# Query and key rows by token tile, with the weights moving, and DMA transposes into head rows

## The chip, the cores and the metric

One NeuronCore of one Trainium2 chip. The metric is the device time of one execution in microseconds (us), from the launch of the kernel to its end; before the change it is 168.42 us, the median of 3 runs (167.94 to 169.54). The profile is of one execution of 168.68 us, in which the instructions span 166.7 us.

The engines are named as in the profile: PE multiplies matrices (PEld is its weight load), DVE and ACT work on vectors, POOL sets up constants, and SP issues most of the DMA transfers. Each runs its own list of instructions in order and waits on semaphores of the others.

## The reference

The input x has 2048 tokens of 448 values, in bfloat16. It is normalised (mean and variance of each token), and two branches read the normalised xn:

```python
# branch A: attention over a dilated window, 16 heads of 28
q, k, v = split(xn @ wqkv)                # [16, 2048, 28] each
idx = pos[:, None] - arange(8)[None] * 2  # 8 keys, every second token back
attn = softmax(where(idx >= 0, q . k[idx] / sqrt(28), -1e9))
s = merge_heads(attn . v[idx]) @ wo
# branch B: feed-forward, 448 -> 1792 -> 448
h = gelu(xn @ w1 + b1) @ w2 + b2
out = x + s * silu(h)
```

Only keys of the same parity are ever used, so the kernel holds the even tokens as positions 0 to 1023 and the odd ones as 1024 to 2047. In this order a query sees the 8 keys up to its own position.

## The kernel before, in words

**Tiling.** Tokens are in 16 tiles of 128 and 4 chunks of 512. The 448 values are contracted in three full tiles of 128 rows and a tail of 64. Two tails share the array at a time, one on its upper 64 rows and one on its lower, which `batch` (line 413) arranges: it closes up to two or more products with their tails and opens others with theirs, in one run of tail matmuls.

**Normalised tokens.** `norm` (390) makes xn for a tile; for the first 8 tiles PE transposes it, from tile 8 on a DMA transpose on the SP queue does it. The result is xnT, with the 448 values on partitions.

**Queries and keys.** `qk` (447) makes the rows for a group of four heads: the stationary operand is a piece of wqk, in which each head's 28 columns are padded to 32 (lines 348 to 357 copy the raw weights wraw into that layout), and the moving one is xnT, with up to 512 tokens. The bank then holds 4 heads x 32 rows by 512 tokens, and ACT or DVE copies it to qT or kT (462), of which there is one tile for each of four head groups. For chunk 0 the moving operand has 256 tokens, for the chunks 1 to 3 all 512.

**Values.** `vproj` (472) works the other way round: the stationary operand is a tile of xnT, the weights move, and tokens come out on partitions, in v_tok. `values` (489) makes the 128 keys of an attention block out of two such tiles by two DMA copies on SP.

**Attention.** `attn` (570) works in 17 blocks of up to 120 queries by 128 keys. The scores are 16 matmuls of 32 rows, which share the array four at a time (580); ACT takes the exponential (586), DVE multiplies with a mask (594), PE multiplies with the values (602), and DVE divides by the sum (609, 614) into os, a ring of three buffers. One or two DMA copies on SP put the block's rows into ot, a ring of four tiles of 128 tokens, and once a tile of tokens is complete a DMA transpose on SP turns it into oT (629).

**Feed-forward and end.** `ff1` (504) is 14 products a chunk with a gelu each, `ff2` (529) is 14 matmuls of 448 columns a tile, then a bias on DVE (552), a tanh on ACT (558) and a product on DVE (562). `final` (635) projects oT with wo, multiplies with the feed-forward branch, adds x and stores.

**What sets the order.** All work is entered as tasks with a cost, what they depend on, buffers they take and give back, and a priority. `_Plan.run` (79) goes through time with these costs and picks for the engine that is free earliest the task of highest priority within 0.12 us; this fixes each engine's list, which then runs in that order whatever the durations on the chip are. A DMA copy within the chip is entered with 0.55 us of SP (`dma_sb`, 309), a DMA transpose with 1.3 (`dma_T`, 315). The priorities are in the table PRIO (704). The chunks are entered in the order of line 739: the feed-forward and the attention of a chunk alternate, since the gelu and the exponential need different tables on ACT.

Of the kernel before, what the change touches and what calls it, by code (L numbers as in the profile page):

```python
# [11 lines left out]
ACT = mybir.ActivationFunctionType  # L12
# [141 lines left out]
def kernel(  # L154
# [46 lines left out]
    def sb(name, shape, dt=BF16):  # L201
        return const.tile(shape, dt, name=name)
# [13 lines left out]
    b1 = sb("b1", [P, NMT], F32)  # L216
    b2 = sb("b2", [P, D])
    xnT = sb("xnT", [P, KT, S])
    qT = [sb(f"qT{g}", [P, S]) for g in range(G)]
    v_tok = [sb(f"v_tok{t}", [P, H, 32]) for t in range(9)]  # L220
    v_tok = v_tok[8:] + v_tok[1:8] + v_tok[:8]
    kT = [sb(f"kT{g}", [P, S]) for g in range(G)]
    oT = sb("oT", [P, KT, S])
    ident = sb("ident", [P, P])
    eps_t = sb("eps_t", [P, 1], F32)
# [30 lines left out]
    def buf(pool, owner, i=0):  # L256
        return pool.bufs[owner.slots[pool][i]]
# [10 lines left out]
    def copy(e, o, i):  # L268
        if e == "ACT":
            nc.scalar.copy(o, i)  # L270
        else:
            nc.vector.tensor_copy(o, i)
# [174 lines left out]
    def qk(t0, t1, g, which, prio):  # L447
        cs = slice(t0 * P, t1 * P)
        n = (t1 - t0) * P
        hs = slice(H * which + 4 * g, H * which + 4 * g + 4)  # L450
        r = slice(64 * which, 64 * which + 64)
        dst, done = (kT, t_k) if which else (qT, t_q)

        def full(ps, kt, start, stop):
            nc.tensor.matmul(ps[:, :n], wqk[:, kt, hs, :], xnT[:, kt, cs], start=start, stop=stop)  # L455

        def tail(ps, start, stop):
            nc.tensor.matmul(ps[:, :n], wqk3[r, 4 * g:4 * g + 4, :], xnT[r, 3, cs], start=start, stop=stop)  # L458

        def evac(a, own, i):  # L460
            def fn(k):
                copy(k.on, dst[g][:, cs], buf(p_b, own, i)[:, :n])
            k = plan.add(("ACT", "DVE"), (act(n), dve(n)), fn, [a], prio + 2, give=((p_b, own, i),))
            for t in range(t0, t1):
                done[(g, t)] = k
        return _Job(n, full, tail, which, [t_xT[t] for t in range(t0, t1)] + t_wqk[:3], evac, (), t_wqk[3:])

    t_v, v_at, h_at = {}, {}, {}
    t_vt = {}
# [100 lines left out]
    def attn(b, prio, gate, early):  # L570
        q0, nq, k0 = BLK[b]
        m = m_b0 if b == 0 else m_sp if b == SPLIT else m_gen
        deps = [t_k[(g, c)] for g in range(G) for c in range(k0 // P, (k0 + P - 1) // P + 1)]
        deps += [t_q[(g, c)] for g in range(G) for c in range(q0 // P, (q0 + nq - 1) // P + 1)]

        def f1(k):
            for g in range(G):
                for hl in range(4):
                    r = slice(32 * hl, 32 * hl + 32)
                    nc.tensor.matmul(buf(p_b, k, hl)[:, g * nq:(g + 1) * nq], kT[g][r, k0:k0 + P],  # L580
                                     qT[g][r, q0:q0 + nq], start=True, stop=True)
        a = plan.add("PE", 0.15, f1, deps + early, prio, take=(p_b,) * 4, tail=0.15, mode=32)
        pv, exps = [], []
        for hl in range(4):
            def f2(k, hl=hl):
                nc.scalar.activation(buf(p_E, k)[:, :, :nq],  # L586
                                     buf(p_b, a, hl)[:, :4 * nq].rearrange("p (g q) -> p g q", g=4),
                                     ACT.Exp, scale=SCALE)
            e = plan.add("ACT", act(4 * nq), f2, [a] + gate + t_E, prio + 2, take=(p_E,), give=((p_b, a, hl),), table=("exp",))
            exps.append(e)  # L590

            def f3(_, e=e):
                E = buf(p_E, e)
                nc.vector.tensor_tensor(out=E[:, :, :nq], in0=E[:, :, :nq], in1=m[:, :, :nq], op=ALU.mult)  # L594
            w = plan.add("DVE", dve(4 * nq, 2), f3, [e] + t_mask, prio + 2)

            def f4(k, e=e, hl=hl):
                ps = buf(p_b, pv[0] if hl else k)[:].rearrange("p (h c) -> p h c", h=H)
                v = buf(*v_at[b]) if v_at[b] else v_tok[k0 // P]
                for g in range(G):  # L600
                    h = 4 * g + hl
                    nc.tensor.matmul(ps[:, h, :DH + 1], buf(p_E, e)[:, g, :], v[:, h, :DH + 1],  # L602
                                     start=True, stop=True)
            pv.append(plan.add("PE", 0.12, f4, [w] + t_v[b] + pv[-1:], prio + 3, take=() if hl else (p_b,),
                               give=((p_E, e, 0),) + ((v_at[b],) if hl == 3 and v_at[b] else ()), tail=0.15))
        po = pv[0]

        def f5(k):
            nc.vector.reciprocal(buf(p_rd, k)[:nq, :],
                                 buf(p_b, po)[:nq, :].rearrange("p (h c) -> p h c", h=H)[:, :, DH])  # L610
        r = plan.add("DVE", 0.25, f5, [pv[-1]], prio + 4, take=(p_rd,))

        def f6(k):
            nc.vector.tensor_tensor(  # L614
                out=buf(p_os, k)[:nq, :].rearrange("p (h c) -> p h c", h=H),
                in0=buf(p_b, po)[:nq, :].rearrange("p (h c) -> p h c", h=H)[:, :, :DH],
                in1=buf(p_rd, r)[:nq, :].unsqueeze(2).to_broadcast((nq, H, DH)), op=ALU.mult)
        o = plan.add("DVE", dve(D), f6, [r], prio + 4, take=(p_os,), give=((p_b, po, 0), (p_rd, r, 0)))
        q = q0
        while q < q0 + nq:  # L620
            t, row = divmod(q, P)
            n = min(P - row, q0 + nq - q)
            first, d = dma_sb(lambda k, t=t, row=row, n=n: buf(p_ot, ot_at.get(t, k))[row:row + n, :D],
                          lambda q=q, n=n: buf(p_os, o)[q - q0:q - q0 + n, :], [o] + t_os + [d for _, d in ot[t]],
                          () if ot[t] else (p_ot,), ((p_os, o, 0),) if q + n == q0 + nq else ())
            ot[t].append((first, d))
            ot_at[t] = ot[t][0][0]
            if row + n == P:
                t_oT[t] = dma_T(oT[:, :, t * P:(t + 1) * P], lambda t=t: buf(p_ot, ot_at[t])[:], [d for _, d in ot[t]],
                                (p_ot, ot_at[t], 0))  # L630
            q += n
        return exps
# [52 lines left out]
    for m, w, n, lo, hi in masks:  # L685
# [13 lines left out]
        def fn(_, m=m, w=w, n=n):  # L699
# [1 line left out]
        t_mask.append(plan.add("DVE", 0.3, fn, [t_m, t_st[3]], prio=60))  # L701


    PRIO = {"project": (77, 71, 71, 36.5),
            "attn": (922.5, 900, 875, 876),
            "ff1": (72.5, 91, 75, 75),
            "ff2": (63, 73, 3, 5),
            "final": (52.5, 36.5, 49.5, 49.5, 93.5, 82.5, 101.5, 48.5)}
    blocks_of = [[b for b, (q0, nq, _) in enumerate(BLK) if (q0 + nq - 1) // CH == c] for c in range(NCH)]
    gate = [early]  # L710

    def project(c):
        p = PRIO["project"][c]
        for t in range(c * TPC, (c + 1) * TPC):
            norm(t, 97 - 2 * t if t < TPC else p + 1)
        vs = [vproj(t, t % 2, p) for t in range(c * TPC, (c + 1) * TPC)]
        if c == 0:
            for i in range(0, len(vs), 2):
                batch(vs[i:i + 1], vs[i + 1:i + 2], 96 if i == 0 else p)
        for t0, t1 in ((0, 2), (2, 4)) if c == 0 else ((c * TPC, (c + 1) * TPC),):  # L720
            for g in (0, 2):
                batch(*[[qk(t0, t1, h, w, p) for w in range(2)] for h in (g, g + 1)], p)
        if c:
            batch(vs[:2], vs[2:], p - 0.1)
        for b in blocks_of[c]:
            values(b)

# [11 lines left out]
    for c, what in ((0, "F"), (0, "A"), (1, "A"), (1, "F"), (2, "A"), (2, "F"), (3, "A"), (3, "F")):  # L739
        if what == "A":  # L740
            exps = []
            for b in blocks_of[c]:
                exps += attn(b, PRIO["attn"][c], gate, gels)
            if c:
                gate = exps
        else:
            p = PRIO["ff1"][c]
            hs = [ff1(c, mt, mt % 2, p, gate) for mt in range(NMT)]
            batch(hs[0:2], hs[2:4], p)
            batch(hs[4:6], hs[6:8], p - 0.01)  # L750
            ff1_last[c] = batch(hs[8:10], hs[10:14], p - 0.02)
            gate = [t_h[(c, mt)] for mt in range(NMT)]
            gels = gate[:-1]
            if c == 0:
                gate = [rstds(8, 8, gate)]
                project(2)
                project(3)
            for t in range(c * TPC, (c + 1) * TPC):
                ff2(t, PRIO["ff2"][c])
    for t in range(NT):  # L760
        final(t, PRIO["final"][t // 2])

    plan.run()
    with tc.manual_schedule():
# [31 lines left out]
```

The softmax here doesn't subtract the row's maximum and nothing guards it: scores larger than these inputs give would overflow.

## Time and profile before

| what | value |
|---|---|
| time, median of 3 | 168.42 us (167.94 to 169.54) |
| span of the profiled execution | 166.7 us |
| DVE busy | 105.2 us (63%) |
| ACT busy | 110.3 us (66%) |
| matmuls for query and key rows, full, 512 columns | 68 x 379 ns = 17.2 us busy (line 455; the trace leaves out a few records) |
| their tails, 512 columns | 24 x 381 ns (line 458) |
| feed-forward 2 matmuls | 224 x 352 ns (line 536) |
| DMA engines, mean share busy by the main queue | 35.6% |

A row of the list of groups reads: line, engine, operation, what is written and read, shapes, count | busy time in us, mean ns of one | idle time of the engine ahead of them, and what ended it. A matmul's duration has its way through the array in it, and matmuls overlap, so the mean of one says less than the pitch at which they follow each other; the chain of work in order of time shows that. Its lines are: start, duration, what, and how many. SPq is SP's list of DMA issues; its durations are what an issue takes the queue, and not how long the data takes.

### The profile page before, as it was taken

To read this page: it belongs to the slowest core of one execution; us is meant where nothing else is said; L and a number is where in the kernel's file an instruction comes from. 1 tells how busy PE (TensorE), PEld (TensorE's weight loads), DVE (VectorE), ACT (ScalarE), POOL (GpSimd) and SP (SyncE) were. 2 spreads that over 40 slices of the span, in tenths; PEclk is the share of its full clock that TensorE was granted. 3 is DMA by queue.
4 is the path that set the end of the run, shared out by engine and by line. 5 is a ranking of instruction groups with operands and counts; after the bars stand their busy time and mean duration, and the time that the engine had idled before them with its cause. 6 is when DMAs were issued, how large, how long until landed. Compare 5 with 4: busy or idle time off the path is not lost.

```text
span 166.7 us, 3522 instructions
## 1 busy us (share of the span) xinstructions
PE 159.5 (96%) x1316; PEld 77.1 (46%) x1328; DVE 105.2 (63%) x278; ACT 110.3 (66%) x201; POOL 4.6 (3%) x29
## 2 busy tenths in 40 slices
PE   6999999999999999999999999999999999999980
PEld 2455534454454455433556533543466543345530
DVE  4789994087899968320196920694788987005762
ACT  3286469987888985698867798454895468851210
POOL 7300000000000000000000000000000000000000
PEclk9999999999999999999999999999999999999996
DMA  5999993024273233235313332022123244100101
GB/s 155 271 374 252 331 304 99 16 50 94 47 93 76 78 82 87 56 97 103 75 37 71 73 66 53 0 83 83 31 75 81 53 130 105 36 0 0 55 28 57
DMA packets 26520, 16.06 MB, mean 96 GB/s; under 512 B 14536, under 2 KB 25992, under 8 KB 26504
## 3 DMA queue, kind: packets, MB, share of 16 engines
q1 hardware_dynamic: 26072, 15.39, 35.6%
q10 hardware_dynamic: 432, 0.46, 0.9%
q8 instruction: 10, 0.16, 0.4%
q14 instruction: 6, 0.05, 0.1%
HBM read 7.06 MB, written 1.84 MB: 53 GB/s over the span
## 4 chain that ended last, share of the span: by engine, by line
PE 91%; DVE 3%; DMA 2%; issue 1%; SPq 1%; DVEq 0%
PE bank L536 25%; PE bank L510 20%; PE bank L455 13%; PE bank L639 7%; PE bank L477 6%; PE bank L602 4%; PE bank L513 4%; PE bank L285 4%; PE bank L580 3%; PE bank L458 3%; DMA ot<-os 2%; PE bank L405 1%; PE bank L480 1%; DVE sg L644 1%; DVE os L614 1%
## 5 line engine op out<-in xcount | busy, mean ns | idle before, releaser
L536 PE MATMUL bank<-w,h 128*128 128x448 bf16 x224 | 46.2, 352 | 0.0
L586 ACT ACTIVATE E<-bank 128x480 bf16<-128x480 f32 (+1 forms) x68 | 33.3, 577 | 10.7 <-PE bank L580 10.6
L510 PE MATMUL bank<-xnT,w 128*128 128x512 bf16 x160 | 38.4, 379 | 0.6 <-issue 0.3
L517 ACT ACTIVATE h<-bank,b 128x512 bf16<-128x512 f32 x56 | 34.3, 700 | 5.1 <-PE bank L513 5.1
L536 PEld LDWEIGHTS <-h 128*128 128x128 bf16 x224 | 20.6, 97 | 18.1
L510 PEld LDWEIGHTS <-w 128*128 128x128 bf16 x168 | 15.1, 97 | 21.6 <-issue 5.8
L455 PE MATMUL bank<-xnT,wqk 128*128 128x512 bf16 (+1 forms) x116 | 24.0, 336 | 0.3 <-issue 0.2
L594 DVE TENSOR_TENSOR E<-E,m_gen 128x480 bf16<-128x480 bf16 x60 | 22.3, 404 | 2.5 <-ACT E L586 1.6
L558 ACT ACTIVATE t<-y 128x448 f32<-128x448 f32 x16 | 9.3, 582 | 18.2 <-DVE y L552 18.1
L552 DVE TENSOR_TENSOR y<-bank,b 128x448 f32<-128x448 f32 x16 | 9.9, 621 | 13.5 <-PE bank L536 13.5
L644 DVE SCALAR_TENSOR_TENSOR sg<-bank,g 128x448 bf16<-128x448 f32 x16 | 9.9, 621 | 9.8 <-PE bank L639 9.2
L602 PEld LDWEIGHTS <-E 128*128 128x128 bf16 x272 | 11.4, 96 | 7.7 <-DVE E L594 0.8
L455 PEld LDWEIGHTS <-wqk 128*128 128x128 bf16 x120 | 10.4, 97 | 8.9 <-issue 2.1
L639 PE MATMUL bank<-wo,oT 128*128 128x448 bf16 x64 | 14.1, 352 | 0.1
L270 ACT CAST qT<-bank 128x512 bf16<-128x512 f32 (+1 forms) x17 | 8.5, 500 | 7.1 <-PE bank L458 5.6
L614 DVE TENSOR_TENSOR os<-bank,rd 120x448 bf16<-120x448 f32 (+1 forms) x17 | 10.6, 625 | 4.0 <-DMA ot<-os 3.4
L602 PE MATMUL bank<-v,E 128*128 128x29 bf16 x240 | 11.2, 176 | 0.0
L365 DVE BATCH_NORM_STATS2 st<-x_sb 128x6 f32<-128x448 bf16 x16 | 9.7, 603 | 1.9 <-DMA x_sb<-in_A_x_dram 1.8
L477 PE MATMUL bank<-wv,xnT 128*128 128x448 bf16 x48 | 10.8, 354 | 0.0
L562 DVE SCALAR_TENSOR_TENSOR g<-t,y 128x448 bf16<-128x448 f32 x16 | 9.9, 620 | 0.9 <-ACT t L558 0.7
L513 PE MATMUL bank<-xnT,w 64*128 64x512 bf16 x56 | 8.8, 380 | 0.1
L639 PEld LDWEIGHTS <-oT 128*128 128x128 bf16 x64 | 5.9, 97 | 5.2
(60 smaller groups left out, 116.0 us busy)
## 6 DMA issues: line engine op xcount, KB each, us to landing
out_dram<-o SPq DMA_DIRECT2D x16, 112.0 KB
w<-in_B_w_dram SPq DMA_DIRECT2D x1, 1568.0 KB
x_sb<-in_A_x_dram SPq DMA_DIRECT2D x3, 448.0 KB
w<-in_B_w_dram SPq DMA_DIRECT2D x1, 1344.0 KB
wraw<-in_A_wqkv_dram SPq DMA_DIRECT2D x1, 448.0 KB
w<-in_B_w_dram SPq DMA_DIRECT2D x2, 224.0 KB
x_sb<-in_A_x_dram SPq DMA_DIRECT2D x3, 112.0 KB
wo<-in_A_wo_dram SPq DMA_DIRECT2D x1, 336.0 KB
```

The source lines that it names most:

```text
L455: nc.tensor.matmul(ps[:, :n], wqk[:, kt, hs, :], xnT[:, kt, cs], start=start, stop=stop)
L477: nc.tensor.matmul(ps[:, :D], xnT[:, kt, k0:k0 + P], wv[:, kt, :], start=start, stop=stop)
L510: nc.tensor.matmul(ps[:], w1[:, kt, ms], xnT[:, kt, cs], start=start, stop=stop)
L513: nc.tensor.matmul(ps[:], w1[r, 3, ms], xnT[r, 3, cs], start=start, stop=stop)
L517: nc.scalar.activation(buf(p_h, own, i)[:], buf(p_b, own, i)[:], ACT.Gelu_apprx_tanh, bias=b1[:, mt:mt + 1])
L536: nc.tensor.matmul(ps[:, :D], buf(*h_at[(c, mt)])[:, j * P:(j + 1) * P], w2[:, mt, :], start=(mt == 0), stop=(mt == NMT - 1))
L586: nc.scalar.activation(buf(p_E, k)[:, :, :nq], buf(p_b, a, hl)[:, :4 * nq].rearrange("p (g q) -> p g q", g=4), ACT.Exp, scale=SCALE)
L594: nc.vector.tensor_tensor(out=E[:, :, :nq], in0=E[:, :, :nq], in1=m[:, :, :nq], op=ALU.mult)
L602: nc.tensor.matmul(ps[:, h, :DH + 1], buf(p_E, e)[:, g, :], v[:, h, :DH + 1], start=True, stop=True)
L614: nc.vector.tensor_tensor(out=buf(p_os, k)[:nq, :].rearrange("p (h c) -> p h c", h=H), in0=buf(p_b, po)[:nq, :].rearrange("p (h c) -> p h ...
L639: nc.tensor.matmul(ps[:, :D], oT[:, kt, t * P:(t + 1) * P], wo[:, kt, :], start=(kt == 0), stop=(kt == KT - 1))
L644: nc.vector.scalar_tensor_tensor(out=buf(p_sg, k)[:], in0=buf(p_b, a)[:, :D], scalar=0.5, in1=buf(p_g, t_g[t])[:], op0=ALU.mult, op1=ALU.mult)
```

## The change

From chunk 1 on, query and key rows are made in the way of the values. The stationary operand is a token tile of xnT, the raw weights wraw move with 448 columns, and a bank then holds 128 tokens by 16 heads x 28. ACT or DVE copies this into a staging buffer of 128 tokens by 16 heads x 32, whose last 4 columns of each head stay zero, and a DMA transpose on SP turns this into the four head groups' rows of 128 tokens. Staging buffers are the six halves of the wqk tile, which after chunk 0 nobody else needs. qT and kT become one tile each, since one transpose writes all four groups. It is to save columns: 448 in place of 512 for each of the matmuls, since the padding no longer passes through PE. Three chunks of 4 tiles with q and k give 24 more DMA transposes; the number of matmuls and of evictions is the same.

The priorities are new too, and finer: of their own for the values, for norm and for the second half of a projection, and by tile for ff2 and final.

```diff
-    qT = [sb(f"qT{g}", [P, S]) for g in range(G)]
+    qT = sb("qT", [P, G, S])
+    kT = sb("kT", [P, G, S])
...
-                copy(k.on, dst[g][:, cs], buf(p_b, own, i)[:, :n])
+                copy(k.on, dst[:, g, cs], buf(p_b, own, i)[:, :n])
...
+    p_qk = _Pool([wqk[:, kt, H * w:H * w + H, :] for kt in range(3) for w in range(2)])
+
+    def qk_rows(t, which, prio):
+        cs = slice(t * P, (t + 1) * P)
+        r = slice(64 * which, 64 * which + 64)
+        dst, done = (kT, t_k) if which else (qT, t_q)
+
+        def full(ps, kt, start, stop):
+            nc.tensor.matmul(ps[:, :D], xnT[:, kt, cs], wraw[:, kt, which * D:(which + 1) * D], start=start, stop=stop)
+
+        def tail(ps, start, stop):
+            nc.tensor.matmul(ps[:, :D], xnT[r, 3, cs], wraw3[r, :], start=start, stop=stop)
+
+        def evac(a, own, i):
+            def fn(k):
+                copy(k.on, buf(p_qk, k)[:, :, :DH], buf(p_b, own, i)[:, :D].rearrange("p (h c) -> p h c", h=H))
+            k = plan.add(("ACT", "DVE"), (act(D), dve(D)), fn,
+                         [a] + [d[g, 0] for d in (t_q, t_k) for g in range(G)] + [d[g, 2] for d in (t_q, t_k) for g in range(G)],
+                         prio + 2, take=(p_qk,), give=((p_b, own, i),))
+            m = dma_T(dst[:, :, cs], lambda: buf(p_qk, k).rearrange("p h c -> p (h c)"), [k], (p_qk, k, 0))
+            for g in range(G):
+                done[(g, t)] = m
+        return _Job(D, full, tail, which, [t_xT[t]], evac)
...
-    PRIO = {"project": (77, 71, 71, 36.5),
-            "attn": (922.5, 900, 875, 876),
-            "ff1": (72.5, 91, 75, 75),
-            "ff2": (63, 73, 3, 5),
-            "final": (52.5, 36.5, 49.5, 49.5, 93.5, 82.5, 101.5, 48.5)}
+    PRIO = {"project": (94.5, 86.5, 66, 41),
+            "attn": (98, 84.5, 65.5, 58.5),
+            "ff1": (94.5, 96.5, 104, 75.5),
+            "ff2": (64.5, 58, 68, 29.5, 80.5, 52, 44.5, 47, 8.5, 5.5, 2, 1.5, 77, 58, 110, 1),
+            "final": (57, 44.5, 9.5, 7.5, 94.5, 55, 84, 67.5, 77.5, 21.5, 75, 54, 16.5, 32.5, 130.5, 50),
+            "values": (15.5, 30.5, 23, 17),
+            "project2": (95.5, 76.5, 26.5, 26.5),
+            "norm": (79.5, 102.5, 10, 1)}
...
-        for t0, t1 in ((0, 2), (2, 4)) if c == 0 else ((c * TPC, (c + 1) * TPC),):
-            for g in (0, 2):
-                batch(*[[qk(t0, t1, h, w, p) for w in range(2)] for h in (g, g + 1)], p)
-        if c:
-            batch(vs[:2], vs[2:], p - 0.1)
+            for t0, t1 in ((0, 2), (2, 4)):
+                for g in (0, 2):
+                    batch(*[[qk(t0, t1, h, w, p) for w in range(2)] for h in (g, g + 1)], p)
+        else:
+            for t, q in ((c * TPC, p), (c * TPC + 2, PRIO["project2"][c])):
+                batch(*[[qk_rows(u, w, q) for w in range(2)] for u in (t, t + 1)], q)
+            batch(vs[:2], vs[2:], pv)
...
-                ff2(t, PRIO["ff2"][c])
+                ff2(t, PRIO["ff2"][t])
...
-        final(t, PRIO["final"][t // 2])
+        final(t, PRIO["final"][t])
```

More of the change, by code (lines that the diff above doesn't have):

```diff
@@ L218 @@
     xnT = sb("xnT", [P, KT, S])
-    qT = [sb(f"qT{g}", [P, S]) for g in range(G)]
+    qT = sb("qT", [P, G, S])
+    kT = sb("kT", [P, G, S])
     v_tok = [sb(f"v_tok{t}", [P, H, 32]) for t in range(9)]
     v_tok = v_tok[8:] + v_tok[1:8] + v_tok[:8]
-    kT = [sb(f"kT{g}", [P, S]) for g in range(G)]
     oT = sb("oT", [P, KT, S])
@@ L579, in f1 @@
                     r = slice(32 * hl, 32 * hl + 32)
-                    nc.tensor.matmul(buf(p_b, k, hl)[:, g * nq:(g + 1) * nq], kT[g][r, k0:k0 + P],
-                                     qT[g][r, q0:q0 + nq], start=True, stop=True)
+                    nc.tensor.matmul(buf(p_b, k, hl)[:, g * nq:(g + 1) * nq], kT[r, g, k0:k0 + P],
+                                     qT[r, g, q0:q0 + nq], start=True, stop=True)
         a = plan.add("PE", 0.15, f1, deps + early, prio, take=(p_b,) * 4, tail=0.15, mode=32)
@@ L712, in project @@
     def project(c):
-        p = PRIO["project"][c]
+        p, pv = PRIO["project"][c], PRIO["values"][c]
         for t in range(c * TPC, (c + 1) * TPC):
-            norm(t, 97 - 2 * t if t < TPC else p + 1)
-        vs = [vproj(t, t % 2, p) for t in range(c * TPC, (c + 1) * TPC)]
+            norm(t, 97 - 2 * t if t < TPC else PRIO["norm"][c])
+        vs = [vproj(t, t % 2, pv) for t in range(c * TPC, (c + 1) * TPC)]
         if c == 0:
             for i in range(0, len(vs), 2):
-                batch(vs[i:i + 1], vs[i + 1:i + 2], 96 if i == 0 else p)
-        for t0, t1 in ((0, 2), (2, 4)) if c == 0 else ((c * TPC, (c + 1) * TPC),):
-            for g in (0, 2):
-                batch(*[[qk(t0, t1, h, w, p) for w in range(2)] for h in (g, g + 1)], p)
-        if c:
-            batch(vs[:2], vs[2:], p - 0.1)
+                batch(vs[i:i + 1], vs[i + 1:i + 2], 96 if i == 0 else pv)
+            for t0, t1 in ((0, 2), (2, 4)):
[5 more added lines that the diff above has]
+            batch(vs[:2], vs[2:], pv)
         for b in blocks_of[c]:
```

## The prediction

> **What bounds the kernel now.** I read the page's busy times and the chain that ended last first, to see which engine sets the span.
>
> ```profile
> PE 159.5 (96%) x1316; PEld 77.1 (46%) x1328; DVE 105.2 (63%) x278; ACT 110.3 (66%) x201; POOL 4.6 (3%) x29
> ...
> PE 91%; DVE 3%; DMA 2%; issue 1%; SPq 1%; DVEq 0%
> ```
>
> PE is busy for all but 7 us, and 91% of the chain is PE. Of those 7 us, 1.2 lie ahead of the first matmul and about 5 behind the last one (from 161.7 to 166.7). What is left between is under 1 us. So a microsecond of matmul taken out is a microsecond of span, as long as nothing makes PE wait that doesn't now.
>
> Second, the chain in order of time, to price a matmul where it runs back to back.
>
> ```profile
> 20.20 0.54 PE bank L513 x4
> 20.74 2.69 PE bank L510 x12
> ...
> 147.51 3.97 PE bank L536 x21
> ```
>
> 21 matmuls of 448 columns take 3.97 us, 189 ns each. Twelve of 512 take 2.69 and the four half-height tails, which run in pairs, 0.54. With a 512 column matmul at 216 ns, twelve make 2.59 and two pairs 0.43, and about 0.1 us is left over in each piece: the price of going from one array tiling to another.
>
> Third, the groups with shapes kept apart, for the query and key rows that are replaced and for the evictions.
>
> ```profile
> L455 PE MATMUL bank<-xnT,wqk 128*128 128x512 bf16 x68 | 17.2, 379 | 0.3 <-issue 0.2
> L270 ACT CAST qT<-bank 128x512 bf16<-128x512 f32 x10 | 5.9, 590 | 5.7 <-PE bank L458 4.4 <-PE bank L455 1.0
> L270 ACT CAST v_tok<-bank 128x448 bf16<-128x448 f32 x9 | 4.8, 539 | 0.6 <-PE bank L480 0.5
> ```
>
> The v_tok row is the price of an eviction of the new kind: 448 columns out of a bank into 16 groups of 28.
>
> Fourth, the DMA queue of SP, since all that is added goes there: durations by tile, and its order of time.
>
> ```profile
> L317 SPq DMA_TRANSPOSE oT<-ot x16: 1190/1216/2109, 42.4 to 140.0; - x16
> ...
> L311 SPq DMA_DIRECT2D v<-v_tok x30: 510/716/1300, 22.5 to 123.0; - x30
> ```
> ```profile
> 34.64 5.23 SPq L317 DMA_TRANSPOSE xnT<-xn  x4
> ...
> 40.32 0.54 SPq L311 DMA_DIRECT2D ot<-os  x1
> 42.40 1.19 SPq L317 DMA_TRANSPOSE oT<-ot  x1
> ...
> 55.64 11.30 SPq L311 DMA_DIRECT2D v<-v_tok  x14
> ...
> 74.62 3.84 SPq L317 DMA_TRANSPOSE oT<-ot  x3
> ```
>
> A transpose holds the queue for 1.22 us and a copy for 0.72; with the gaps I use 1.25 and 0.74. From 34.6 to 80.4 us the queue's pieces add up to 40.4 of 45.8 us: PE is not the only thing that is nearly full. Its lateness already reaches an engine, in the list of waits:
>
> ```profile
> DVE os L614 <- DMA ot<-os: 3.4, 1, 3.4
> ```
>
> At 68.3 us DVE stood still for 3.4 us until a copy had freed an os buffer. PE was in a feed-forward stage then and did not need DVE, so it cost nothing.
>
> **What the Trainium skill says.** "TensorE: Matmul & The Clock Gate", section Back-to-back issue gap, gives N/2.4 + 2.5 ns for an isolated warm matmul and says that a real stream runs closer. Here the formula holds: it gives 189 ns for 448 columns (189 measured) and 216 for 512 (216 fits). "Perfetto Trace Analysis", section DMA Instruction — HWDGE (DVE, Sync), says that the profiler's window of such an instruction covers the sequencer and the descriptors, and not the movement of the data. The trace agrees: the first transpose is issued at 34.64, the DMA engines are empty until 35.85, and busy until 36.6, so it lands some 2.2 us after its issue began. "DMA: Bandwidth & Descriptors", section Issuing engines are not separate DMA queues, says that spreading DMAs over queues saves only issue time; no run here shows it, but issue time is what is scarce.
>
> **The change part by part.**
>
> *Matmuls.* A chunk has 24 full and 8 tail matmuls of 512 columns before, and as many of 448 after. A full one saves 64/2400 = 26.7 ns; the tails run in pairs, so count as 4. That is 28 x 26.7 = 0.747 us a chunk, 2.24 us for three. In the changed order PE goes from one tiling to another 88 times against 87, which gives 0.1 back. Gain: 2.14 us.
>
> *Evictions.* There are 24 either way. Before: 5.9 + 4.7 us on ACT (10 qT, 8 kT), 4.1 on DVE. After: 19 on ACT at 0.54 and 5 on DVE at 0.62, 13.4 against 14.7 us. Both engines have a third of the span free; I count nothing.
>
> *One tile for all head groups, the new weights.* The scores read the same 32 rows by 120 columns, and the raw weights have long landed, since the padded layout is copied out of them before its first use at 9.5 us: nothing.
>
> *Transposes on the DMA engines.* 24 of 0.13 MB. The four of 34.6 to 40.5 ran at about 220 GB/s, 0.6 us each, so 24 make 14 us over 90 us of span, beside engines that are a third busy: not a bound. Landing time: q and k of a tile come 2.2 us after the issue, before the evictions alone. The scores of block 4 stand in PE's order some 13 us behind the first of these evictions, so that is hidden.
>
> *Transposes on the SP queue.* This is the cost. Sixteen of them (chunks 1 and 2) fall into the stretch that was 40.4 of 45.8 us full, and 16 x 1.25 = 20 us don't fit. So what the queue did there slips. I walk the queue in the changed order, from the first xn transpose, which starts near 34.6 in both: the matmuls ahead of it are the same. Ahead of the transpose of the first attention output tile (oT 0) stand 24 transposes and 23 copies: 24 x 1.25 + 23 x 0.74 = 47.0, and 0.8 for the third xn, which DVE makes after a y and a mask product. So oT 0 is issued at 82.4 and lands at 84.6. Three more transposes, and at 86.2 to 86.9 the copy that lets go of os1; it lands some 1.4 us after its issue (40.86 to 42.40 is 1.5), at 88.3. The copy that lets go of os2 follows after a transpose and three copies, at 90.4, and lands at 91.8.
>
> PE, by the same prices and the changed order, counted from the start of feed-forward 0 at 18.91 + 0.93 (16 norm transposes of 58 ns now come ahead of it) and with what the same count falls short of the trace before (0.8 us at 60, 1.3 at 79): block 5's values are wanted at 59.8, output projection 0 at 84.0, the second head group's product of block 9 at 87.5. Against the queue:
>
> - Blocks 5 and 6 need value copies that stand 23rd and 24th in the queue, land at 60.4 and 61.2, and find PE at 59.8 and 60.5. PE waits about 1 us in all. Output projection 0 then comes at 85.0, just after oT 0.
> - DVE's order has block 7's normalisation into os1 ahead of a g and the mask product of block 9's second group. It waits to 88.3; os 0.65, g 0.6, product 0.4 end at 90.0. PE stands at 88.5: 1.5 us.
> - The same at os2: 91.8, then 0.6 and 0.4 give 92.8, PE at 92.0: 0.8. The products behind it cost 0.4 and 0.2.
>
> Then the queue has room: a block brings one transpose and two copies, 2.7 us, and PE takes over 4 for a block with its feed-forward work. In the last chunk I find no wait over 0.4, and leave it out. New waits: 1.0 + 1.5 + 0.8 + 0.6 = 3.9 us.
>
> *Priorities.* They only change the order, which the walk has in it. The end is the same in both orders (14 feed-forward matmuls, 8 of the projection, then DVE and the last store), so the 5 us tail stays.
>
> Sum: 168.42 - 2.14 + 3.9 = 170.2 us. The two bounds for the waits: nothing, if each copy finds 1 us of slack more at each place; and with a transpose at 1.6 us in a burst (two at 46.0 took 3.25) the queue is 24 x 0.35 = 8.4 us later at oT 0, of which PE, being later too, would feel 5 to 7 us in place of 3.9. I take the median prices, because most bursts show them.
>
> **The rivals.**
>
> *The queue keeps up.* PE gets its 2.14 us and waits for nothing: 166.3. For it: the new order puts the attention transposes and stores late and the q and k ones early, as if the queue had been reckoned with, and the 3.4 us wait of DVE before cost nothing. Against it: the 60 us of issue for 46 us.
>
> *The queue runs at burst prices.* 168.42 - 2.14 + 6.5 = 172.8. For it: transposes of 1.93 and 2.11 us in dense stretches. Buffers add to it: an eviction into one of the six staging buffers waits for a transpose six earlier, on ACT, with exponentials queued behind it, whose banks PE wants. Against it: of 24 transposes few are over 1.3.
>
> **How the numbers follow.** The late queue, 170.2, has 0.48; it spreads over 168.5 to 171.7. The queue that keeps up, 166.3, has 0.32, and burst prices, 172.8, 0.20. Faster by over 1% (below 166.7) is most of the second, 0.28; within 1% is the rest of it and the lower part of the first, 0.29; slower (above 170.1) 0.43. The range from 166.0 to 173.0 holds both rivals' middles.
>
> **What would show it.** Right: 48 transposes on SP at about 1.2 us, the queue without gaps from 35 to 85 us, PE busy near 157.3, DVE os waiting for ot copies between 80 and 95 us, with PE weight loads of E waiting for DVE there. Wrong: PE at its old 96% with 2 us less, so that the queue's lateness found slack; or PE waiting for kT or qT, which I hold to be in time; or ACT waiting at the staging buffers.

## The result and the profile after

The changed kernel takes 176.81 us (median of 4, 175.97 to 177.35) against 168.37 for the one before in the same comparison: a ratio of 1.0485, with an interval of 1.0418 to 1.0552. It is slower by 8.4 us, where 1.8 had been forecast, and outside the range. The profiled execution took 175.97 us, with a span of 174.2 us against 166.7. Here and below a time is the median of all executions, and a ratio leaves out the slow ones, which lie over 1.5% above the fastest of the same kernel.

The page of the kernel after: busy times, two rows of the 40 slices, the chain by engine, the two groups of matmuls that now stand still, and the new rows' full matmuls and evictions on ACT.

```profile
PE 159.8 (92%) x1320; PEld 77.1 (44%) x1328; DVE 103.3 (59%) x276; ACT 110.1 (63%) x203; POOL 4.5 (3%) x29
...
PE   7999999999999679999849999999898999999980
...
PEclk9999999999999999999996999999999999999998
...
PE 75%; DMA 8%; SPq 7%; DVE 5%; issue 2%; ACT 1%; DVEq 0%
...
L664 PE MATMUL bank<-wo,oT 128*128 128x448 bf16 x64 | 14.2, 352 | 3.2 <-DMA oT<-ot 3.2
...
L627 PE MATMUL bank<-v,E 128*128 128x29 bf16 x240 | 11.6, 176 | 3.3 <-DMA v<-v_tok 3.0
...
L477 PE MATMUL bank<-wraw,xnT 128*128 128x448 bf16 x72 | 16.1, 352 | 0.0
...
L270 ACT CAST wqk<-bank 128x448 bf16<-128x448 f32 x19 | 9.7, 548 | 4.1 <-PE bank L480 2.9
```

PE was 91% of the chain and is 75%; DMA and SP's queue together were 3% and are 15%. PE waits 3.2 us for the first attention output (oT) and 3.0 for the value copies, and in one slice its clock is down to 0.6. The new matmuls (L477) wait for nothing, and an eviction takes 0.55 us, as was reckoned (0.54).

PE's order of time in the kernel after, cut to the pieces from 30 us on with a wait of over 0.2 us (start, us, what, how many; in brackets the idle time ahead and what ended it), and three that show the slow clock:

```profile
59.51 0.56 PE L627 MATMUL bank<-v,E 128*128 128x29 bf16 x16 [1.55 <-DMA v<-v_tok]
...
62.06 0.90 PE L627 MATMUL bank<-v,E 128*128 128x29 bf16 x20 [0.84 <-DMA v<-v_tok]
...
84.22 1.48 PE L561 MATMUL bank<-w,h 128*128 128x448 bf16 x7
...
89.58 0.93 PE L664 MATMUL bank<-wo,oT 128*128 128x448 bf16 x4 [3.17 <-DMA oT<-ot]
90.35 2.52 PE L561 MATMUL bank<-w,h 128*128 128x448 bf16 x7
...
92.81 2.09 PE L561 MATMUL bank<-w,h 128*128 128x448 bf16 x7
...
126.31 0.56 PE L627 MATMUL bank<-v,E 128*128 128x29 bf16 x16 [0.64 <-DMA v<-v_tok]
...
135.19 0.39 PE L605 MATMUL bank<-qT,kT 32*128 32x120 bf16 x16 [0.68 <-DMA kT<-wqk]
```

Every one of these waits is for something that SP issues. Seven feed-forward matmuls take 1.48 us before the long wait, and 2.52 and 2.09 after it.

SP's queue in order of time:

```profile
34.84 3.91 SPq L317 DMA_TRANSPOSE xnT<-xn  x3
...
42.12 1.22 SPq L317 DMA_TRANSPOSE qT<-wqk  x1
43.43 1.22 SPq L317 DMA_TRANSPOSE kT<-wqk  x1
...
47.04 1.97 SPq L317 DMA_TRANSPOSE kT<-wqk  x1
49.11 1.21 SPq L317 DMA_TRANSPOSE qT<-wqk  x1
...
57.43 6.38 SPq L311 DMA_DIRECT2D v<-v_tok  x8
...
85.55 4.83 SPq L317 DMA_TRANSPOSE oT<-ot  x3
```

From 34.8 to 90 us the gaps between its pieces are only some 0.1 us. oT 0 is issued at 85.55 us; PE had come to its projection at 86.41 (89.58 less 3.17). By tile (shortest, median, longest issue in ns, first and last start):

```profile
L317 SPq DMA_TRANSPOSE oT<-ot x16: 1204/1222/2192, 85.5 to 152.9; - x16
...
L311 SPq DMA_DIRECT2D v<-v_tok x30: 521/724/887, 21.0 to 129.2; - x30
```

The medians are those of before (1.22 and 0.72). The first attention output is transposed at 85.5 where it had been at 42.4. Its place in SP's list comes from the plan with the 24 transposes in it: with the new rows and the old priorities (kernel 4 below) it is issued at 84.7, with the new priorities and the old rows (kernel 3) at 44.0.

The wait of DVE for the os buffers, in the list of waits (total, times, longest), was one of 3.4 us and is now:

```profile
DVE os L639 <- DMA ot<-os: 2.9, 2, 1.5
```

### The profile page after: what moved, and what is told of

The parts are those of the page before. It is cut to its first block, busy times and chain, and to the rows that moved or that the text cites. A ratio compares the mean times of both kernels' runs of the same rounds, so it can differ in the third digit from the quotient of the medians.

```text
span 174.2 us, 3554 instructions
## 1 busy us (share of the span) xinstructions
PE 159.8 (92%) x1320; PEld 77.1 (44%) x1328; DVE 103.3 (59%) x276; ACT 110.1 (63%) x203; POOL 4.5 (3%) x29
## 4 chain that ended last, share of the span: by engine, by line
PE 75%; DMA 8%; SPq 7%; DVE 5%; issue 2%; ACT 1%; DVEq 0%
PE bank L535 21%; PE bank L561 18%; PE bank L477 7%; PE bank L502 5%; PE bank L664 5%; PE bank L538 4%; SPq L317 4%; PE bank L627 3%; PE bank L455 3%; SPq L311 3%; DMA wraw<-in_A_wqkv_dram 3%; PE bank L605 3%; DMA v<-v_tok 2%; PE bank L480 2%; DMA kT<-wqk 1%
## 5 line engine op out<-in xcount | busy, mean ns | idle before, releaser
L561 PE MATMUL bank<-w,h 128*128 128x448 bf16 x224 | 47.6, 361 | 0.0
L611 ACT ACTIVATE E<-bank 128x480 bf16<-128x480 f32 (+1 forms) x68 | 33.3, 580 | 19.2 <-PE bank L605 16.7
L477 PE MATMUL bank<-wraw,xnT 128*128 128x448 bf16 x72 | 16.1, 352 | 0.0
L634 DVE RECIPROCAL rd<-bank 120x16 f32<-120x16 f32 (+1 forms) x17 | 4.4, 256 | 17.3 <-PE bank L627 17.1
L270 ACT CAST wqk<-bank 128x448 bf16<-128x448 f32 x19 | 9.7, 548 | 4.1 <-PE bank L480 2.9
L538 PE MATMUL bank<-xnT,w 64*128 64x512 bf16 x56 | 8.1, 380 | 0.0
```

Of the source, the lines that this page charges most:

```text
L477: nc.tensor.matmul(ps[:, :D], xnT[:, kt, cs], wraw[:, kt, which * D:(which + 1) * D], start=start, stop=stop)
L538: nc.tensor.matmul(ps[:], w1[r, 3, ms], xnT[r, 3, cs], start=start, stop=stop)
L561: nc.tensor.matmul(ps[:, :D], buf(*h_at[(c, mt)])[:, j * P:(j + 1) * P], w2[:, mt, :], start=(mt == 0), stop=(mt == NMT - 1))
L611: nc.scalar.activation(buf(p_E, k)[:, :, :nq], buf(p_b, a, hl)[:, :4 * nq].rearrange("p (g q) -> p g q", g=4), ACT.Exp, scale=SCALE)
```

## The experiments

The theory after the result: the queue of SP is overfull, and all that is lost is PE waiting for what the queue issues late. Rivals: the new priorities are a worse order in themselves; the data that the transposes move is in the way; the slow clock after the long wait is a large part.

| kernel | time, us | ratio to before, interval | oT 0 issued at, us |
|---|---|---|---|
| after | 176.81 | 1.0485 (1.0418 to 1.0552) | 85.6 |
| 1: no transposes, rows set to zero | 178.17 | 1.0568 (1.0514 to 1.0621) | |
| 2: all copies on POOL | 166.91 | 0.9905 (0.9876 to 0.9935) | 73.7 |
| 3: priorities alone | 174.40 | 1.0343 (1.0290 to 1.0396) | |
| 4: rows with the old priorities | 178.97 | 1.0626 (1.0559 to 1.0693) | 84.7 |
| 5: no transposes, scores read chunk 0 | 166.85 | 0.9890 (0.9870 to 0.9911) | 78.3 |
| 6: PE kept warm at the wait | 177.94 | 1.0551 (1.0516 to 1.0587) | 86.8 |
| 7: kernel before, copies on POOL | 167.72 | 0.9935 (0.9914 to 0.9956) | |
| 8: planner told a dearer copy | 174.78 | 1.0361 (1.0327 to 1.0395) | 87.8 |
| 9: value copies alone on POOL | 167.05 | 0.9915 (0.9893 to 0.9936) | 75.6 |
| 10: row copies alone on POOL | 169.12 | 1.0039 (1.0023 to 1.0056) | 81.6 |
| 11: keys not transposed | 168.02 | 0.9974 (0.9957 to 0.9991) | 80.4 |
| 12: planner told of POOL's queue | 172.70 | 1.0243 (1.0154 to 1.0332) | |

Where an edit has no other base named, it is one to the kernel after.

### The transposes taken out (1 and 5)

Kernel 1 leaves the 24 query and key transposes out, and sets the rows of chunks 1 to 3 to zero.

```diff
+    t_zq = [plan.add("POOL", 0.0, memset("gpsimd", q[:, :, CH:], 0.0), [t_on], prio=1) for q in (qT, kT)]
...
-            m = dma_T(dst[:, :, cs], ..., [k], (p_qk, k, 0))
+            m = dma_T(dst[:, :, cs], ..., [k], (p_qk, k, 0), skip=True)
```

> The changed kernel with its 24 query and key transposes left out and all else in the same order on each engine (queries and keys of the chunks 1 to 3 are then zeros, so this part of the computation is missing). Theory, the SP queue is overfull: without the 24 issues of 1.3 us PE loses its waits for value copies, for the first output tile and for keys, and the slow clock behind one of them; it has the 2.1 us of columns less than before: 166 to 168 us. Rival, the new order itself (priorities) makes PE wait: 173 us or more. Rival, 448 column matmuls with a token tile standing still do not run faster than 512 ones: 168.5 to 170 us, with PE pitch near 216 ns in the projection.

Measured: 178.17 us. The edit brought a delay of its own. DVE's order of time at the start of kernel 1:

```profile
5.58 10.49 DVE L398 COPY xn<-xn 128x64 bf16<-128x64 bf16 x1
...
16.56 0.18 DVE L398 COPY xn<-xn 128x64 bf16<-128x64 bf16 x1
```

A copy that takes 0.18 us took 10.49 while POOL ran the two memsets, of 5.22 us each, and PE stood still for 9.7 us. Nothing follows from the time. Kernel 5 does the same without a memset: the transposes are left out, and the scores of all blocks read the rows of chunk 0.

```diff
-                    nc.tensor.matmul(..., kT[r, g, k0:k0 + P], qT[r, g, q0:q0 + nq], ...)
+                    nc.tensor.matmul(..., kT[r, g, k0 % 384:k0 % 384 + P], qT[r, g, q0 % 384:q0 % 384 + nq], ...)
```

> The 24 transposes left out once more, without the two memsets of POOL that held DVE up for 10 us at the start of the first try: the scores of all blocks read chunk 0's queries and keys (so the attention of the chunks 1 to 3 is computed from wrong rows). Order on every engine as in the changed kernel. Theory, issue time on SP: 165.5 to 168 us, PE idle under 2 us between 20 us and its last matmul. Rival, the order: 173 us or more.

Measured: 166.85 us, span 164.8. The order of instructions is that of the kernel after, so the two traces can be laid side by side. PE's order of time in kernel 5, at the places where the kernel after waits first:

```profile
57.89 0.56 PE L629 MATMUL bank<-v,E 128*128 128x29 bf16 x16
...
83.39 0.92 PE L666 MATMUL bank<-wo,oT 128*128 128x448 bf16 x4
84.15 1.49 PE L563 MATMUL bank<-w,h 128*128 128x448 bf16 x7
...
87.08 0.39 PE L607 MATMUL bank<-qT,kT 32*128 32x120 bf16 x16
```

The delay of the kernel after against kernel 5, piece by piece (starts on PE in us, blocks counted from 0):

| piece of PE | kernel 5 | after | behind | added, and by what |
|---|---|---|---|---|
| scores of block 6 | 57.57 | 57.57 | 0 | |
| scores of block 7 | 62.04 | 64.91 | 2.87 | 2.87, value copies of blocks 4 and 5 |
| first projection | 83.39 | 89.58 | 6.19 | 3.32, oT 0 |
| scores of block 10 | 87.08 | 94.92 | 7.84 | 1.65, slow clock and DVE behind os |
| scores of block 13 | 115.48 | 123.09 | 7.61 | -0.23 |
| scores of block 14 | 118.38 | 126.81 | 8.43 | 0.82, value copies |
| scores of block 15 | 125.86 | 135.19 | 9.33 | 0.90, keys |
| last projection | 158.30 | 167.63 | 9.33 | 0 |

The spans differ by 9.4. So in this order the transposes cost all of it, and without them the new order and the fewer columns give 1.9 us of span under the kernel before (166.7 less 164.8). The rival of the priorities as a cause by themselves is out: the same order runs at 166.85. PE's busy time in kernel 5:

```profile
PE 157.3 (95%) x1328; PEld 76.4 (46%) x1328; DVE 103.0 (63%) x276; ACT 109.9 (67%) x203; POOL 4.4 (3%) x29
```

### Room on the queue, with the transposes kept (2, 9, 10, 7)

Kernel 2 keeps the plan and its order, and lets POOL issue the 61 copies.

```diff
-            nc.sync.dma_start(dst(k), src())
+            nc.gpsimd.dma_start(dst(k), src())
```

> The changed kernel with the copies within the chip (values and attention rows, 61 of them) issued from the POOL queue in place of SP's; bytes, transposes and the order within each engine stay. Theory, issue time on SP: SP holds only transposes, first output tile issued some 15 us earlier, no PE wait of 3 us and no slow clock; 167 to 171 us, depending on what an issue from POOL costs. Rival, the DMA engines themselves are overfull with the 24 transposes' data: no better than 174 us, since the same bytes move in the same stretch.

Measured: 166.91 us. The page of kernel 2, and two pieces of its order of time, on PE and on SP:

```profile
PE 157.5 (95%) x1328; PEld 76.5 (46%) x1328; DVE 103.1 (62%) x276; ACT 110.0 (67%) x203; POOL 37.3 (23%) x90
```
```profile
84.70 0.92 PE L664 MATMUL bank<-wo,oT 128*128 128x448 bf16 x4
```
```profile
67.46 6.16 SPq L317 DMA_TRANSPOSE xnT<-xn  x4
73.73 18.20 SPq L317 DMA_TRANSPOSE oT<-ot  x7
```

oT 0 is issued 11.8 us sooner than in the kernel after, and PE's waits are down to 0.64 and 0.33 us, both near 60. All transposes move their data here, and none of the 24 does in kernel 5; both take the same time. The data is not in the way; the issuing is. POOL's copies also run in a DMA queue of their own, so the edit changes more than the issuing. But in the kernel after the DMA engines were busy for only 0.36 to 0.49 of the time from 40 to 86 us, so little can have stood behind other data.

Kernels 9 and 10 divide it: only the 30 value copies on POOL, or only the 31 copies of attention rows.

```diff
-        a, d1 = dma_sb(lambda k: buf(p_v, k)[:P - r], ..., (p_v,))
+        a, d1 = dma_sb(lambda k: buf(p_v, k)[:P - r], ..., (p_v,), eng="gpsimd")    # 9, and so for d2
...
-                          () if ot[t] else (p_ot,), ((p_os, o, 0),) if q + n == q0 + nq else ())
+                          () if ot[t] else (p_ot,), ((p_os, o, 0),) if q + n == q0 + nq else (), eng="gpsimd")    # 10
```

> The changed kernel with only the 30 value copies issued from the POOL queue; the 31 copies of attention rows and all transposes stay on SP, every other order too. Theory, SP is short of issue time: 22 us less of it from the first value copy of chunk 1 on, so the waits for values, the first output tile and the last key go: 166.5 to 168.5 us. Rival, only part of the lateness comes from the queue's sum, the rest from long transposes and landing times: 170 to 174 us.

> The changed kernel with only the 31 copies of attention rows issued from the POOL queue; the value copies stay on SP. Theory, the sum of the queue: about 7 us less ahead of the first output tile, which is as much as that tile was late, and 5 of it ahead of the first value copy: 166.5 to 169 us. Rival, the value copies have to leave SP since eight of them come in one burst: the wait of 2.9 us near 58 us stays, 170 us or more.

Measured: 167.05 and 169.12 us. With the value copies away PE waits once, 0.64 us for keys. With the row copies away the value copies come in time (the first at 54.2 in place of 57.4), but 0.49 us for oT 0, and 0.64 and 0.75 for DVE's products, stay. Sixteen of the value copies stand ahead of oT 0, and only seven of the row copies, so taking the value copies off SP frees its queue more where it matters.

Kernel 7 does to the kernel before what 2 does to the one after (the same edit).

> The kernel before with its 61 copies within the chip issued from the POOL queue, as in the second experiment, and nothing else. Theory, the queue of SP cost PE nothing before the change: within 1% of before, 167 to 170 us; then the gain of the second experiment over before is the columns' 2 us. Rival, the POOL queue is better for any kernel: 166 us or less.

Measured: 167.72 us, a little under the kernel before. With the copies on POOL on both sides the change takes 167.7 to 166.9 us, or by the ratios 0.9935 to 0.9905. That would be 0.5 to 0.8 us, but the two intervals overlap, so no gain of the change is shown there; 0.65 of the 0.95% by which kernel 2 is under the kernel before come with POOL alone. Kernels 2 and 9 are the fastest that compute the whole result, about 1% under the kernel before, and their intervals overlap too.

### Half the transposes (11)

Twelve, those of the keys, left out; scores read the keys of chunk 0.

```diff
+            m = dma_T(dst[:, :, cs], ..., [k], (p_qk, k, 0), skip=bool(which))
```

> The changed kernel with the 12 transposes of keys left out and the 12 of queries kept (all blocks read chunk 0's keys, so the attention of the later chunks is computed from wrong keys). Theory, the queue has a limit, and lateness below it is taken up by slack: less than a third of the 10 us of all 24 remains, 167 to 169.5 us. Rival, each transpose costs PE its share: 171 to 172.5 us.

Measured: 168.02 us. Half of the transposes cost 1.2 of the 10 us, the other half the other 8.8: oT 0 is issued at 80.4, 5.2 us sooner, and lands before PE asks. The first half finds room in the queue. The second takes 15.6 us of SP's time (12 at the 1.30 us worked out below), and PE feels more than half of it. Of the two waits left, 1.52 and 0.35 us, the first is told of below.

### Priorities (3 and 4)

Kernel 3 makes the query and key rows in the old way with the new priorities, kernel 4 the new rows with the old ones.

```diff
-            for t, q in ((c * TPC, p), (c * TPC + 2, PRIO["project2"][c])):
-                batch(*[[qk_rows(u, w, q) for w in range(2)] for u in (t, t + 1)], q)
+            for g, q in ((0, p), (2, PRIO["project2"][c])):
+                batch(*[[qk(c * TPC, (c + 1) * TPC, h, w, q) for w in range(2)] for h in (g, g + 1)], q)
```

> The kernel before in all its projections (512 tokens moving, no transposes added), with the changed kernel's table of priorities and its single qT and kT tiles. Theory, the transposes are the cause: within 2 us of before, 167 to 171 us. Rival, the priorities are the cause: 173 us or more.

> The changed kernel's projections by token tile and their transposes, with the priorities of the kernel before. Theory, the queue is overfull whatever the order: slower than before, 172 to 182 us, with waits of PE for what SP brings. Rival, the priorities are the cause: 165.5 to 168 us.

Measured: 174.40 and 178.97 us. Taken alone, kernel 3 speaks for the rival: its number came. But kernel 5 has the very order of the kernel after and runs at 166.85. So the new priorities are slow with the old rows, and fast with the new ones where the queue is not short. Why kernel 3 is slow is not followed to the end: none of PE's waits there is for a transfer of SP's, it waits 1.1 and 1.2 us for DVE's mask products (107.8 and 141.5 us), and its clock falls after the first. Kernel 4 shows what the new priorities do for the new rows. Its list of waits:

```profile
DVE os L639 <- DMA ot<-os: 19.1, 2, 18.2
```

Here DVE stands 18.2 us for an os buffer, and PE 3.89 behind it. In the new order the same wait is 2.9 us.

### The slow clock (6)

Twelve matmuls on zeros go into the first projection's bank ahead of it, where PE would stand still.

```diff
+            if t == 0:
+                for _ in range(12):
+                    nc.tensor.matmul(ps[:], warm[:, :P], warm[:], start=True, stop=True)
```

> The changed kernel with 12 matmuls on zeros put ahead of output projection 0, into its own bank, where PE stood idle for 3.2 us; all else in the same order. Theory, the idle stretch makes the clock slow for some 3.5 us after it: PE clock stays at full speed there and the time falls by 1.5 to 2 us, to 174.8 to 175.3. Rival, the slow clock has another cause: no gain, or 2.6 us more.

Measured: 177.94 us, not less than the kernel after. The windows of both (from:to, us, then PE, PEld, DVE, ACT and POOL busy, the clock, DMA share, GB/s), after first, then kernel 6:

```profile
90.00:92.00 2.00, 2.00 (x9) 0.89 (x8) 0.63 (x1) 0.00 (x0) 0.00 (x0) 0.66 0.46 99
92.00:94.00 2.00, 2.00 (x11) 0.88 (x10) 1.38 (x3) 0.00 (x0) 0.00 (x0) 0.50 0.40 82
```
```profile
90.00:92.00 2.00, 1.22 (x7) 0.68 (x8) 0.25 (x1) 0.00 (x0) 0.00 (x0) 1.00 0.64 123
92.00:94.00 2.00, 2.00 (x16) 1.09 (x15) 0.69 (x2) 0.00 (x0) 0.00 (x0) 1.00 0.51 111
94.00:96.00 2.00, 1.24 (x28) 0.62 (x27) 1.47 (x4) 0.17 (x1) 0.00 (x0) 1.00 0.29 80
```

The clock stays full, and PE then waits 0.76 and 0.59 us for DVE's products, which stand behind the late os buffers. From the first projection to the scores of block 11 it is 9.2 us in the kernel after and 9.1 here. At this place the slow clock cost nothing of its own: PE ran slowly through time in which it would have waited. Kernel 6 is longer for reasons elsewhere: of its 1.5 us more of span (175.7 against 174.2) 1.0 are there at 60 us, ahead of the edit, where the first wait for value copies is 2.20 us in place of 1.55, and 0.4 come at the keys of block 15 (1.10 in place of 0.68).

### The planner told better (8 and 12)

Kernel 8 enters a copy at 0.78 us in place of 0.55. Kernel 12 puts the copies on POOL, as kernel 2, and tells the planner of it, so the order is made anew.

```diff
-        a = plan.add("SP", 0.55, fn, deps, 75, take=take)
+        a = plan.add("SP", 0.78, fn, deps, 75, take=take)        # 8
+        a = plan.add("POOL", 0.55, fn, deps, 75, take=take)      # 12, with nc.gpsimd.dma_start
```

> The changed kernel planned with 0.78 us for a copy on SP in place of 0.55, so that the planner knows the queue's true speed; this gives another order on every engine. Theory, the plan is late because it underrates the queue: 170 to 174 us, with PE idle for DMA below 3 us. Rival, the price in the plan does not matter since the load is the same: 176 us or more.

> The changed kernel with all 61 copies issued from POOL, and planned so: the copies take POOL's time and no longer SP's. This gives another order on every engine, with the same priorities. Theory, what is short is SP's issue time, and a planner that knows of a second queue has no reason to put off what waited for it: 165 to 167.5 us, PE idle under 2 us behind 20 us. Rival, the priorities were chosen for the plan with one queue and suit no other, as in the third experiment: 170 us or more.

Measured: 174.78 and 172.70 us, both above what was expected. A truer price gives back 2 of the 10 us; oT 0 is issued even later, at 87.8, PE's wait for it is 1.72, and waits for DVE's products take the place. Kernel 12 is worse than kernel 2 by 5.8 us with the same queues. From its list of waits, and from POOL's and PE's pieces:

```profile
POOL ot L311 <- DMA oT<-ot: 23.7, 3, 16.7
```
```profile
58.71 1.09 POOL L311 DMA_DIRECT2D v<-v_tok  x2 [0.36 <-issue]
...
62.45 0.55 PE L627 MATMUL bank<-v,E 128*128 128x29 bf16 x16 [2.33 <-issue]
```

POOL stands up to 16.7 us, until 86 us, at a row copy whose ot tile is not yet read, but PE waits for nothing in that stretch, so this is not shown to cost anything. PE's longest wait is 2.33 us at 62.45. The list names no releaser; by their place the value copies that POOL issued from 58.71 us on are likely, and from 60 to 64 us the DMA engines were full (share 1.0 and over). The rest of the difference is not followed. With priorities that were not made for it, a planner that knows more did not do better here.

## Why the prediction failed, point by point

**The columns: right in PE's time.** 2.14 us was the forecast. PE's busy time goes from 159.5 (its trace lacks 12 of 1328 matmuls) to 157.3 in kernel 5, and the span from 166.7 to 164.8. Between kernels 7 and 2, with all records on both sides, it goes from 159.2 to 157.5, but the span only from 165.7 to 165.3; kernel 2 waits 0.97 us near 60 us, where kernel 7 does not.

**Data, staging buffers: right.** Kernels 2 and 5 agree; at the staging buffers, where one rival had ACT wait, the list of the kernel after names only DVE, with 0.3 us. (In kernel 4, with the old priorities, ACT waits 3.8 us there.)

**What the queue does: right in kind.** It runs without gaps, DVE waits for os, PE for what comes late. Wrong is the size of "New waits: 3.9 us": it is 9.3. Its terms:

| place | forecast | measured | the step that failed |
|---|---|---|---|
| value copies, 60 us | 1.0 | 2.9 | the queue's pace |
| oT 0 | 0 | 3.3 | pace, and the landing |
| os1, os2 and behind | 2.9 | 1.4 | too large: PE came later itself |
| last chunk | 0, left out | 1.7 | "I find no wait over 0.4" |

*The pace.* "24 x 1.25 + 23 x 0.74 = 47.0, and 0.8" is the step. From the first xn transpose to oT 0 the trace has 50.7 us: 31.2 for the transposes, 1.30 each; 17.3 for the copies, 0.75 each; 2.3 between pieces. The walk had taken medians of durations with next to nothing for gaps; in a row the transposes follow each other at 1.31 us (42.12 to 43.43), and two of the 24 were long, 1.97 and 1.54. The 0.8 us for the third xn did not show: the three take 3.91 us in a row. So oT 0 is issued at 85.55 and not 82.4, and the value copies begin at 57.43, where the walk gives 34.6 + 0.8 + 13 x 1.25 + 6 x 0.74 = 56.1. Block 4's copy, the first of them, which the walk held in time, came 1.55 us late; block 5's landed at 62.06 and not at 60.4.

*The landing.* oT 0 was to land 2.2 us after its issue, as the first transpose of a group did in the kernel before. It took 4.0 (85.55 to 89.58). Pace and landing make oT 0 late by 5.0 us against the walk's 84.6; 0.4 of it was slack, PE came 1.4 later than the walk's 85.0, and the wait is 3.2.

*The last chunk.* The walk stopped where "the queue has room". Late value copies cost 0.8 at 126.3 us, and the keys of block 15 0.9 at 135.2: "PE waiting for kT or qT, which I hold to be in time" was named as a sign of error, and it came.

**The bounds.** The upper one came from the issue price alone: it let the queue be 8.4 us late and PE feel 6.5. The queue was only 3.1 us late against the walk at oT 0, and PE lost 9.3: being late already by 2.9 from the value copies did not spare it 3.3 more at oT 0, nor 1.7 in the last chunk. Lateness at one place did not bound the loss over all. The rival at burst prices, 172.8, was the nearest, but for a reason that did not hold: of the 24 transposes ahead of oT 0 only the two named were over 1.4 us.

**Not foreseen:** the half clock after the wait, which by kernel 6 cost nothing of its own at that place.

In the forecast's own terms, -2.14 + 3.9 us was expected, and -1.9 + 9.4 us of span measured.

## What to carry to other kernels

Before moving work to DMA, add up what the issuing queue has to do in the stretch where its results are wanted, at the pitch of issues in a row and not at the median duration, and add the slowest landing seen to the last item. The cost does not grow evenly: while the queue has room, more work is nearly free (half of the transposes cost 1.2 us here), and once it is full, much of the time goes to the critical engine (the other half cost 8.8 us for 15.6 us of issue). When it is full, let another engine with time to spare issue a part, and keep the order of the rest as it is.

## What the runs showed of the hardware that was not expected

**Transfers that meet a small instruction load land some 2 us later.** The DMA windows of the kernel after at the landing of oT 0 (86.5 to 89.6 us), and of kernel 11 at its one long wait (56.0 to 59.6): GB/s in 40 slices, and the instruction queue's packets.

```profile
GB/s 0 0 0 268 145 208 188 221 192 221 188 109 47 3 0 0 0 0 0 10 7 7 10 10 10 10 7 13 10 20 0 0 17 63 159 215 201 235 185 235
...
q8 instruction: 1, 0.02, 2.5%
```
```profile
GB/s 3 1 0 0 0 0 0 216 171 216 262 228 103 12 0 0 11 148 171 57 23 0 0 0 11 0 11 11 11 11 11 0 11 11 23 0 68 171 160 114
...
q8 instruction: 1, 0.02, 2.7%
```

In both, one packet of 16 KB for an engine's instructions comes among the first (2.5% of 16 engines for 3.1 us is 1.2 us of one engine), most of the transfer passes at about 200 GB/s, and then mostly 7 to 13 GB/s trickle for about a microsecond. PE is let go after that, at 89.58 and 59.60. The landing takes 4.0 us in place of 2.2, and 4.1 (55.51 to 59.60) in place of 2.1 (57.43 to 59.51). In kernel 6 the packet is there as well, and oT 0 takes 3.95 us (86.83 to 90.78); in kernel 8 there is none at this place, and it takes 2.5 (87.76 to 90.25). It looks as if one DMA engine's share of the transfer stood behind the packet. The long issues on SP (47.04, 69.96, 86.87, 122.49 and 136.23 us in the kernel after) come with such packets too. That is a coincidence seen many times; no run took the packets away, so the cause stays open. The kernel before has them at the same places (58 and 86 us), with nobody waiting.

**Issuing was not small beside the transfer.** "DMA: Bandwidth & Descriptors", section Issuing engines are not separate DMA queues, which the prediction named, calls the time saved by a second issuing engine usually small relative to the DMA itself. Here a transpose took 1.22 us to issue and about 0.6 to move (0.13 MB at about 220 GB/s), and moving the copies to POOL saved 9.9 us of 177 (kernel 2). POOL's issue of a copy took 0.54 us where SP's took 0.72. Its landing was not faster: in kernel 2 a value copy landed 4.1 us after its issue in the median.

**The clock can halve without a long standstill of PE.** "TensorE: Matmul & The Clock Gate", section What's actually happening, gives half clock after an idle window of about 3.4 us, which runs freely. In the kernel after it was 0.50 behind 3.2 us of idling, close to that. In kernel 3 it fell to 0.50 between 109 and 110 us, behind 2 us with PE busy for 0.66 and 2 with 1.78 in which PE stood for about 1.1 us at the longest, so the window need not be wholly idle.

**A memset on POOL can stop DVE.** "SBUF — State Buffer", section SBUF: two separate sides, says that DVE in some of its modes and GpSimd share a port, which one holds for its whole instruction. Kernel 1 agrees: 10.5 us for a DVE copy of 0.18, behind two memsets of 5.2.
